# Scores of a windowed attention in eight 64x32 parts of the TensorE array, 96 keys at a time, from the third tile on

## The chip, the cores and the metric

The kernel runs on one core of one Trainium2 chip. The metric is the device time of one execution in microseconds (us). Inputs and outputs lie in the chip's memory; the host only lays the arrays out before the launch.

## What is computed

Attention over a sliding window, and a gated feed-forward layer on its output, all in float32:

```python
# q, k, v: (8 batches, 8 heads, 576 positions, 64)
scores = (q @ k.T) / sqrt(64)
mask   = (rel >= 0) & (rel < 64)            # rel = query position - key position
attn   = softmax(where(mask, scores, -1e9))
x      = (attn @ v) as 4608 tokens x 512    # the heads side by side
out    = ((sigmoid(x @ w_gate) * (x @ w_val)) @ w_out)   # 512 -> 1536 -> 512
```

A query sees itself and the 63 keys before it. So the 64 queries of one block need the keys of their own block and of the block before: 128 keys. In this 64 x 128 piece of scores only a band is kept. Its first 32 queries have nothing to keep among the last 32 keys, and its last 32 queries nothing among the first 32.

## The kernel before, in words

The 4608 tokens are cut into ten tiles: two of 384, six of 512, two of 384 (`SIZES`). A tile `t` has four pairs of heads `p` (two heads side by side on 128 partitions). One such pair in one tile is called a unit here; a unit of a 512-token tile has eight blocks of 64 queries, one of a 384-token tile six.

For each unit, `scores` multiplies each block of 64 queries with its 128 keys, for both heads: a contraction over 64 rows, 64 output rows, 128 columns. Such a product takes one quarter of the array (a 64x64 part). The four products of two neighbouring blocks and two heads lie on four different quarters and write two PSUM banks, one for each head: the row half `h` of the array always writes bank `sc[h]`. The products are float32, and the trace holds two matmul records, each with a weight load of its own, for each of them. A unit of 512 tokens thus has 32 records ahead of anything else, one of 384 tokens 24.

After the scores, VectorE reads each 128 x 128 piece from PSUM, adds a mask, scales it and takes the row minimum in one instruction (line 275, 128 columns always). ScalarE takes the exponential (line 290). Rows are divided by their sums, TensorE transposes the result (lines 382 and 395), and `outputs` multiplies it with v (line 425).

Around this runs the feed-forward layer. The first two tiles take the plain way (lines 457 and 498). The other eight go two at a time through a scheme with seven products in place of eight (`PRODUCTS`, line 659), with three instructions per product that multiply high and low parts of the operands. The weights are made in the first third of the run, written to the chip's memory and read back for each pair of tiles.

The order of TensorE's instructions is written out by hand: `put(time, order, function, ...)` fills a list of events that is sorted by time, and `pe(...)` keeps TensorE's instructions in program order. The other engines' order is planned by a list scheduler that runs a model of the timeline; `tc.issue_after` adds single constraints.

The attention of the first two tiles is done at the start, before the feed-forward layer has anything to work on. Attention of tiles three and four is done in pairs of units between the plain feed-forward stages (`near_s`, `near_h`, `near_o`). That of the later tiles is done in twelve visits of two units between the products (`far_visits`, `stage_s`). So `scores` for `t > 1` is called for two units back to back, 16 times in all: 12 times for two units of 512 tokens (64 records) and 4 times for two units of 384 tokens (48 records).

All eight PSUM banks come from pools: six with tags `b00` to `b12`, one buffer each, and one pool with two buffers (`ps_a`), which the scores, the transposed weights and some outputs share. In a visit the first unit's scores go to banks `b11` and `b01`, the second's to the two buffers of `ps_a`; the second product after the visit needs `b11` and `b01` again.

Of the kernel before, what the change touches and what calls it, by code (L numbers as in the profile page):

```python
# [9 lines left out]
F32 = mybir.dt.float32  # L10
# [6 lines left out]
PSUM = bass.MemoryType.PSUM  # L17

P = 128
BLK = 64  # L20
SMALL, BIG = 384, 512
SIZES = [SMALL] * 2 + [BIG] * 6 + [SMALL] * 2
FIRST = [sum(SIZES[:i]) for i in range(len(SIZES))]
# [2 lines left out]
def tt(t):  # L26
    return SIZES[t]


def ut(t):  # L30
    return tt(t) // BLK


def up2(t):
    return ut(t) // 2
# [3 lines left out]
def attn_ffn(ctx: ExitStack, tc: tile.TileContext, qT, kT, vS, vB, w_gate, w_val, w_out, out, outT):  # L39
# [3 lines left out]
    nc = tc.nc  # L43
    DM = out.shape[1]
    D = BLK
    NF = w_gate.shape[0]
# [5 lines left out]
    NS = NT // 2  # L52
    J_AT = [j // 2 + (j % 2) * NK for j in range(NF)]
    SCALE = 1.0 / math.sqrt(D)
    NEG = -1e9 / SCALE
    H = DM // 2
    WB, HB, RAW, CB, GB = 9, 10, 3, 3, 4
    SLOTS = 17 * 2 * BIG
# [7 lines left out]
    sm = ctx.enter_context(tc.tile_pool(name="sm", bufs=4))  # L66
    dr = ctx.enter_context(tc.tile_pool(name="dr", bufs=1, space=bass.MemoryType.DRAM))
    ps_b = ctx.enter_context(tc.tile_pool(name="ps_b", bufs=1, space=PSUM))
    ps_a = ctx.enter_context(tc.tile_pool(name="ps_a", bufs=2, space=PSUM))


    masks = {key: const.tile([P, P], F32, name=f"m_{key[0]}{key[1]}") for key in ((0, 0), (1, 0), (0, 1))}
# [2 lines left out]
    for h in range(2):  # L75
        rows = band[h * BLK:(h + 1) * BLK]
        nc.gpsimd.affine_select(out=rows, in_=rows, pattern=[[1, P]], compare_op=ALU.is_ge,
                                fill=NEG, base=-1, channel_multiplier=-1)
        nc.gpsimd.affine_select(out=rows, in_=rows, pattern=[[-1, P]], compare_op=ALU.is_ge,
                                fill=NEG, base=BLK, channel_multiplier=1)  # L80
    for h, key in enumerate(((1, 0), (0, 1))):
        nc.vector.tensor_copy(out=masks[key], in_=band)
        rows = masks[key][h * BLK:(h + 1) * BLK]
        nc.gpsimd.affine_select(out=rows, in_=rows, pattern=[[1, P]], compare_op=ALU.is_ge,
                                fill=NEG, base=-BLK, channel_multiplier=0)
    ident = const.tile([P, P], F32, name="ident")
# [2 lines left out]
    nc.vector.memset(warm, 0.0)  # L89
    nc.scalar.activation(warm, warm, AF.Exp)  # L90

    def psum(s, i, nm):
        return ps_b.tile([P, DM], F32, name=nm, tag=f"b{s % 2}{i}")

    marks = {"pT": {}}
    chain = []
# [11 lines left out]
    def pe(ins):  # L108
        return tc.keep_in_program_order(ins)
# [101 lines left out]
    def bank(t, p, n, nm):  # L211


        i = NP * t + p
        if t < 2 and i < 2 * NP - 1 and (n[0] != "s" or i % 2):
            s, x = {"s0": (0, 0), "s1": (0, 1), "p0": (1, 0), "p1": (1, 1), "o": (1 - i % 2, 2)}[n]
            return blocks(psum(s, x, nm), t)
        return blocks(ps_a.tile([P, DM], F32, name=nm, tag="a"), t)

    def blocks(bank, t):  # L220
        return bank[:, :tt(t)].rearrange("p (u c) -> p u c", u=up2(t))

    def stage_a(t, p):
        scores(t, p)
        softmax(t, p)

    def scores(t, p):
        qt, kt = ld.pop((t, p))
        if (t, p) not in sc_of:
            sc_of[(t, p)] = [bank(t, p, f"s{h}", f"s{h}_{t}_{p}") for h in range(2)]  # L230
        if (t, p) == (0, 0):
            rest = [blocks(psum(1, h, f"sb{h}_{t}_{p}"), t) for h in range(2)]
            sc_of[(t, p)] = [[x[:, 0, :]] + [y[:, u, :] for u in range(1, up2(t))] for x, y in zip(sc_of[(t, p)], rest)]
        else:
            sc_of[(t, p)] = [[x[:, u, :] for u in range(up2(t))] for x in sc_of[(t, p)]]
        sc = sc_of[(t, p)]
        for u in range(up2(t)):
            for s in range(2):
                U = 2 * u + s
                for h in range(2):  # L240
                    half = s ^ h
                    pe(nc.tensor.matmul(sc[h][u][half * BLK:(half + 1) * BLK, :],  # L242
                                     qt[h * BLK:(h + 1) * BLK, U * BLK:(U + 1) * BLK],
                                     kt[h * BLK:(h + 1) * BLK, U * BLK:U * BLK + P], start=True, stop=True))

    def softmax(t, p):
        sc = sc_of.pop((t, p))
        for h in range(2):
            exponentials(t, p, h, sc[h])
            if t < 2:  # L250
                total(t, p, h)
            else:
                normalize(t, p, h)
        if t < 2:
            stage_n(t, p)
# [53 lines left out]
    def stage_s(units, done):  # L309
        xo = []  # L310
        for i, (t, p) in enumerate(done):
            xo.append(outputs(t, p, blocks(psum(1 - i, 0, f"ob{i}_{t}_{p}"), t)))
        for i, (t, p) in enumerate(units):
            if i == 0:
                sc_of[(t, p)] = [blocks(psum(1 - h, 1, f"s{h}_{t}_{p}"), t) for h in range(2)]
            scores(t, p)
            if i == 0:
                for (dt, dp), oo in zip(done, xo):
                    x_copy(dt, dp, oo)
        if not units:  # L320
            for (dt, dp), oo in zip(done, xo):
                x_copy(dt, dp, oo)
        for i, (t, p) in enumerate(units):
            sc = sc_of.pop((t, p))
            for h in range(2):
                mn = exponentials(t, p, h, sc[h], i > 0)
                if i:
                    mn_of[(t, p, h)] = mn
# [11 lines left out]
    def by_block(x, t):  # L340
        return x[:, :tt(t)].rearrange("p (h u c) -> p h u c", h=2, u=up2(t))
# [7 lines left out]
    def near_s(units, late):  # L349
        for i, (t, p) in enumerate(units):  # L350
            if i == 0:
                sc_of[(t, p)] = [blocks(spare_bank(late, h, f"s{h}_{t}_{p}"), t) for h in range(2)]
            scores(t, p)
        for t, p in units:
            sc = sc_of.pop((t, p))
            for h in range(2):
                mn_of[(t, p, h)] = exponentials(t, p, h, sc[h], True)
# [8 lines left out]
    def near_h(units, late):  # L366
        by_halves(units, lambda r, nm: spare_bank(late, r, nm))
# [4 lines left out]

    def by_halves(units, extra=lambda r, nm: psum(1 + r, 0, nm)):
        for i, (t, p) in enumerate(units):
            pp = [extra(r, f"pp{r}_{t}_{p}") if i else ps_a.tile([P, DM], F32, name=f"pp{r}_{t}_{p}", tag="a")
                  for r in range(2)]
            for h in range(2):
                pt = st[(t, p, h)]
                for u in range(up2(t)):
                    for r in range(2):  # L380
                        rows = slice(r * BLK, (r + 1) * BLK)
                        pe(nc.tensor.transpose(by_block(pp[r], t)[:, h, u, :], pt[rows, u, :], ident[rows, rows]))  # L382
            for r in range(2):
                pT = st[(t, p, r)].rearrange("p u c -> p (u c)")
                marks["pTv"] = nc.scalar.copy(pT, pp[r][:, :tt(t)]).ins
                st[(t, p, r)] = by_block(pT, t)
            halved.add((t, p))

    def stage_b(t, p):
        UP = up2(t)  # L390
        for h in range(2):
            pt = st[(t, p, h)]
            pp = bank(t, p, f"p{h}", f"pp{h}_{t}_{p}")
            for u in range(UP):
                pe(nc.tensor.transpose(pp[:, u, :], pt[:, u, :], ident))  # L395
            if t < 2:
                pT = mp.tile([P, SMALL], F32, name=f"pT{h}_{t}_{p}", tag="g", bufs=GB).rearrange("p (u c) -> p u c", u=UP)
            else:
                pT = pt
            cp = nc.scalar.copy(pT, pp)  # L400
            marks["pTv"] = cp.ins
            if t < 2:
                marks["pT"][NP * t + p] = cp.ins
            st[(t, p, h)] = pT
# [384 lines left out]
    for n in range(2 * NP):  # L789
        t, p = divmod(n, NP)  # L790
# [123 lines left out]
    for s in range(1, NS):  # L914
# [58 lines left out]
        if s < NS - 1:  # L973
            for n in range(NPR):
                for c in range(2):
                    x = 2 * n + c
# [87 lines left out]
```

## Time and profile before

| | |
|---|---|
| median of 3 runs | 921.94 us (921.76 to 922.63) |
| span of the profiled execution, first to last instruction | 919.5 us |
| what lies around the span, against the median | 2.4 us |
| PE (TensorE matmul) busy | 907.5 us, 99% of the span |
| VectorE (DVE) busy | 679.5 us, 74% |
| ScalarE (ACT) busy | 476.1 us, 52% |

The page gives no whole time for the profiled execution beside its span, so the span stands against the median of the three runs. A busy share of TensorE near 100% says only that its queue never ran dry; how fast its matmuls follow each other has to be read stretch by stretch. Times within a trace are in us from the first instruction.

### The profile page before, as it was taken

The numbers are of one execution on the slowest core, as the hardware profiler recorded it, in microseconds if no ns is written. First come the engines' busy times: TensorE is split into PE (matmuls) and PEld (weight loads), VectorE is DVE, ScalarE is ACT, GpSimd is POOL, SyncE is SP. The second block draws the span as 40 slices with busy tenths as digits, with TensorE's granted clock in tenths as the row PEclk, the third lists the DMA queues.
The fourth block names the chain that finished last, engine by engine and source line by source line (L and its number), as shares of the span: only waits on it lengthen the run. The fifth ranks groups of instructions, "written<-read, shape, count | busy, mean of one in ns | idle before, by whom it ended". The sixth has DMA issues, their size and how long they took to land.

```text
span 919.5 us, 18434 instructions
## 1 busy us (share of the span) xinstructions
PE 907.5 (99%) x6584; PEld 788.6 (86%) x6584; DVE 679.5 (74%) x1689; ACT 476.1 (52%) x1208; POOL 129.6 (14%) x204
## 2 busy tenths in 40 slices
PE   6999999999999999999999999999999999999998
PEld 5899999888888888888888888888888888999998
DVE  7887878578898899947666698656655986565881
ACT  7867858554466677525554355424442454222550
POOL 4200000087653402001111100001110000000000
PEclk9999999999999999999999999999999999999999
DMA  9899999679989967787676665766755558888783
GB/s 338 313 406 354 359 324 358 203 244 338 345 315 331 336 241 264 253 270 243 236 233 218 206 189 193 263 217 227 228 188 172 202 187 254 270 252 251 256 256 107
DMA packets 92107, 240.02 MB, mean 261 GB/s; under 512 B 9968, under 2 KB 20080, under 8 KB 92016
## 3 DMA queue, kind: packets, MB, share of 16 engines
q1 hardware_dynamic: 91728, 238.62, 76.1%
q8 instruction: 52, 0.85, 0.4%
q14 instruction: 39, 0.32, 0.1%
q10 hardware_dynamic: 288, 0.23, 0.1%
HBM read 186.91 MB, written 51.90 MB: 260 GB/s over the span
## 4 chain that ended last, share of the span: by engine, by line
PE 97%; ACT 2%; DMA 0%; DVE 0%; issue 0%; SPq 0%; DVEq 0%; ACTq 0%
PE pr L659 47%; PE y L659 23%; PE ph L457 11%; PE y L498 6%; PE s L242 3%; PE ob L425 2%; PE pp L382 1%; PE oo L425 1%; PE pp L395 1%; ACT p L290 1%; DMA k<-in_kT_dram 0%; ACT pT L400 0%; DVE p L275 0%; SPq L195 0%; ACT w L171 0%
## 5 line engine op out<-in xcount | busy, mean ns | idle before, releaser
L659 PE MATMUL pr<-slots,wt 128*128 128x512 f32 (+1 forms) x1728 | 373.8, 375 | 0.0
L659 PEld LDWEIGHTS pr<-slots,wt 128*128 128x128 f32 x1728 | 315.3, 188 | 49.3 <-issue 1.7
L659 PE MATMUL y<-slots,wot 128*128 128x512 f32 (+1 forms) x1008 | 215.8, 375 | 0.0
L659 PEld LDWEIGHTS y<-slots,wot 128*128 128x128 f32 x1008 | 185.5, 188 | 29.6 <-issue 0.2
L465 ACT ACTIVATE g<-c 128x512 f32<-128x512 f32 (+1 forms) x72 | 43.6, 606 | 156.8 <-DVE c L698 154.5
L737 ACT CAST slots<-h 128x512 fp32r<-128x512 f32 (+1 forms) x144 | 83.7, 595 | 71.7 <-PE y L659 41.7
L290 ACT ACTIVATE p<-p,mn 128x128 f32<-128x128 f32 x288 | 108.0, 391 | 22.9 <-DVE mn L275 22.8
L738 DVE TENSOR_TENSOR slots<-h,slots 128x512 fp32r<-128x512 f32 (+1 forms) x144 | 92.9, 666 | 19.4 <-ACT slots L737 18.9
L457 PE MATMUL ph<-slots,w 128*128 128x384 f32 x576 | 104.7, 337 | 0.0
L457 PEld LDWEIGHTS ph<-slots,w 128*128 128x128 f32 x576 | 100.1, 188 | 2.1 <-DVE w L172 0.3
L305 POOL TENSOR_TENSOR p<-p,rs 128x384 f32<-128x384 f32 (+1 forms) x47 | 43.5, 946 | 346.9 <-DVE rs L298 330.7
L659 PE MATMUL pr<-slots,ws 128*128 128x512 f32 x288 | 68.3, 391 | 0.0
L669 DVE TENSOR_TENSOR c<-pr,p 128x512 f32<-128x512 f32 (+1 forms) x48 | 31.4, 655 | 45.0 <-PE pr L659 44.9
L275 DVE CUSTOM_DVE_ANT_0 p<-s,m 128x128 f32<-128x128 f32 x284 | 62.5, 285 | 1.6 <-PE s L242 1.6
L659 PEld LDWEIGHTS pr<-slots,ws 128*128 128x128 f32 x288 | 53.8, 188 | 11.0
L470 DVE SCALAR_TENSOR_TENSOR h<-g,c 128x512 f32<-128x512 f32 (+1 forms) x72 | 48.7, 676 | 6.1 <-DVE c L698 0.5
L498 PE MATMUL y<-w,slots 128*128 128x512 f32 x216 | 52.7, 396 | 0.0
L669 DVE TENSOR_TENSOR u<-pr,p 128x512 f32<-128x512 f32 (+1 forms) x48 | 31.1, 654 | 27.6 <-PE pr L659 14.8
L649 ACT CAST slots<-xf 128x512 fp32r<-128x512 f32 (+1 forms) x48 | 27.9, 598 | 40.5 <-PE y L659 31.7
L498 PEld LDWEIGHTS y<-w,slots 128*128 128x128 f32 x216 | 39.8, 188 | 8.8 <-issue 0.7
L698 DVE TENSOR_TENSOR c<-pr,p 128x512 f32<-128x512 f32 (+1 forms) x48 | 31.2, 654 | 21.3 <-PE pr L659 21.1
L290 ACT ACTIVATION_READ_ACCUMULATOR p<-p,mn 128x1 f32 x240 | 45.1, 188 | 0.0
(93 smaller groups left out, 980.7 us busy)
## 6 DMA issues: line engine op xcount, KB each, us to landing
wt<-wd SPq DMA_DIRECT2D x144, 512.0 KB, 4.3
wot<-wod SPq DMA_DIRECT2D x84, 512.0 KB, 4.2
v<-in_vB_dram SPq DMA_DIRECT2D x24, 512.0 KB, 5.5
wd<-ws SPq DMA_DIRECT2D x48, 256.0 KB, 4.5
w32d<-w SPq DMA_DIRECT2D x36, 256.0 KB, 5.4
wd<-w SPq DMA_DIRECT2D x36, 256.0 KB, 6.1
out_dram<-yo SPq DMA_DIRECT2D x30, 256.0 KB, 5.0
k<-in_kT_dram SPq DMA_DIRECT2D x24, 288.0 KB, 6.3
```

Of the source, the lines that this page charges most:

```text
L275: nc.vector.tensor_tensor_reduce(out=pt[:, u, :], in0=sc[u], in1=masks[key], op0=ALU.add, op1=ALU.min, scale=-SCALE, scalar=3.0e38, accum_ ...
L290: exp = nc.scalar.activation(pt[:, u, :], pt[:, u, :], AF.Exp, bias=mn[:, u:u + 1], scale=-1.0, **sums)
L305: eng.tensor_mul(out=pt, in0=pt, in1=rs.unsqueeze(2).broadcast_to([P, up2(t), P]))
L457: pe(nc.tensor.matmul(ph, l, r, start=i == 0 and 0 in parts, stop=i == len(prs) - 1 and NP - 1 in parts))
L465: act = nc.scalar.activation(g, c, AF.Tanh)
L470: nc.vector.scalar_tensor_tensor(out=out, in0=g, scalar=1.0, in1=val, op0=ALU.add, op1=ALU.mult)
L498: pe(nc.tensor.matmul(yb[y], l, r, start=first and n == 0, stop=last and n == 2))
L659: pe(nc.tensor.matmul(ps, l, r, start=first and i == 0, stop=last and i == 2, skip_group_check=not check))
L669: marks["plus"] = nc.vector.tensor_add(out=o, in0=ps, in1=a).ins
L698: nc.vector.tensor_add(out=c, in0=in0, in1=in1)
L737: nc.scalar.copy(h2[:, 0, :], src)
L738: lo = nc.vector.tensor_sub(out=h2[:, 1, :], in0=src, in1=h2[:, 0, :].bitcast(F32))
```

## The change

Three things are changed.

1. `scores` for `t > 1` calls `scores_by_32`. Each block of 64 queries is cut into two halves of 32, and each half is multiplied with 96 keys only: the first half with the first 96 of the 128, the second with the last 96. Each product has 32 output rows and so takes one eighth of the array (a 64x32 part). Two blocks, two heads and two halves lie on eight different parts. The 32 x 32 corners that are not written keep what the bank held before.
2. The mask value goes from -8e9 to -1e30, so that whatever lies in a corner comes out as zero after the exponential.
3. The PSUM banks are no longer taken from pools again and again. Eight tiles are made once and looked up by name; `psum_a` takes `a0` and `a1` in turn. VectorE fills the columns from 384 on of each bank with zeros at the start (eight new instructions of 128 x 128), so that nothing undefined lies there.

```diff
+Q = 32
...
-    NEG = -1e9 / SCALE
+    NEG = -1e30
...
-    ps_a = ctx.enter_context(tc.tile_pool(name="ps_a", bufs=2, space=PSUM))
...
+    banks = {x: ps_b.tile([P, DM], F32, name=f"ps_{x}") for x in [f"b{s}{i}" for s in range(2) for i in range(3)] + ["a0", "a1"]}
+    for x in banks.values():
+        nc.vector.memset(x[:, SMALL:], 0.0)
+    turn = [-1]
+
     def psum(s, i, nm):
-        return ps_b.tile([P, DM], F32, name=nm, tag=f"b{s % 2}{i}")
+        return banks[f"b{s % 2}{i}"]
+
+    def psum_a(nm):
+        turn[0] += 1
+        return banks[f"a{turn[0] % 2}"]
...
-        return blocks(ps_a.tile([P, DM], F32, name=nm, tag="a"), t)
+        return blocks(psum_a(nm), t)
...
         sc = sc_of[(t, p)]
+        if t > 1:
+            scores_by_32(t, qt, kt, sc)
+            return
...
+    def scores_by_32(t, qt, kt, sc):
+        W = P - Q
+        for u in range(up2(t)):
+            for i in range(2):
+                for s in range(2):
+                    for h in range(2):
+                        r0, c0 = (s ^ h) * BLK + i * Q, (2 * u + s) * BLK + i * Q
+                        pe(nc.tensor.matmul(sc[h][u][r0:r0 + Q, i * Q:i * Q + W], qt[h * BLK:(h + 1) * BLK, c0:c0 + Q],
+                                            kt[h * BLK:(h + 1) * BLK, c0:c0 + W], start=True, stop=True))
...
-            pp = [extra(r, f"pp{r}_{t}_{p}") if i else ps_a.tile([P, DM], F32, name=f"pp{r}_{t}_{p}", tag="a")
+            pp = [extra(r, f"pp{r}_{t}_{p}") if i else psum_a(f"pp{r}_{t}_{p}")
```

## Rows read from the trace of the kernel before

**Rows 1.** The page: busy time by engine, and the chain by line.

```profile
span 919.5 us, 18434 instructions
PE 907.5 (99%) x6584; PEld 788.6 (86%) x6584; DVE 679.5 (74%) x1689; ACT 476.1 (52%) x1208; POOL 129.6 (14%) x204
...
PE pr L659 47%; PE y L659 23%; PE ph L457 11%; PE y L498 6%; PE s L242 3%; PE ob L425 2%; PE pp L382 1%; PE oo L425 1%; PE pp L395 1%; ACT p L290 1%; DMA k<-in_kT_dram 0%; ACT pT L400 0%; DVE p L275 0%; SPq L195 0%; ACT w L171 0%
```

**Rows 2.** The chain in order of time: start, us, what.

```profile
2.12 4.39 DMA k<-in_kT_dram
...
6.64 1.62 PE s L242 x24
...
57.18 1.91 PE s L242 x64
...
244.76 1.91 PE s L242 x64
246.67 8.43 PE pr L659 x36
...
342.75 2.02 PE ob L425 x64
344.77 1.91 PE s L242 x64
...
500.13 1.47 PE s L242 x48
...
640.66 1.55 PE ob L425 x48
...
665.65 1.47 PE s L242 x48
```

**Rows 3.** Timeline of PE in three short windows around 344.70, 344.87, 345.02 us.

```profile
344.70 0.34 PE L242 MATMUL s<-k,q 64*64 64x128 f32 x4
...
344.70 0.45 PE L242 MATMUL s<-k,q 64*64 64x128 f32 x8
...
344.70 0.56 PE L242 MATMUL s<-k,q 64*64 64x128 f32 x12
```

**Rows 4.** Groups by line and shape, PE: busy us, mean ns, idle before.

```profile
L242 PE MATMUL s<-k,q 64*64 64x128 f32 x1136 | 38.9, 283 | 4.8 <-DMA k<-in_kT_dram 4.6 <-DVE rs L298 0.3
L425 PE MATMUL ob<-p,v 128*64 128x64 f32 x704 | 23.2, 224 | 0.0
```

**Rows 5.** Waits in PE's queue, lines L242 (27.50 to 27.57) and L425 (27.77 to 27.80).

```profile
L242 PEldq EVENT_SEMAPHORE  x1: 51/51/51, 27.6 to 27.6; - x1
...
L425 PEldq EVENT_SEMAPHORE  x1: 51/51/51, 27.8 to 27.8; - x1
```

**Rows 6.** Timeline of all engines, first microseconds.

```profile
0.73 0.20 POOL L74 MEMSET m<- 128x128 f32 x1 [0.29 <-POOLq L1050]
...
0.80 0.06 DVE L89 MEMSET warm<- 128x1 f32 x1 [0.80 <-PEq L1050]
...
2.64 0.46 DVE L82 COPY m<-m 128x128 f32<-128x128 f32 x2 [1.77 <-POOL m L79]
...
3.21 0.70 PE L242 MATMUL s<-k,q 64*64 64x128 f32 x8 [3.21 <-DMA k<-in_kT_dram]
...
4.08 0.29 DVE L275 CUSTOM_DVE_ANT_0 p<-s,m 128x128 f32<-128x128 f32 x1 [0.99 <-PE s L242]
```

**Rows 7.** Busy time by engine in stretches; columns PE, PEld, DVE, ACT, POOL, clock, DMA.

```profile
244.80:269.80 25.00, 25.00 (x232) 21.00 (x236) 24.80 (x70) 16.41 (x51) 15.13 (x27) 1.00 0.90 313
269.80:294.80 25.00, 25.00 (x232) 21.03 (x236) 22.44 (x65) 15.32 (x50) 10.56 (x20) 1.00 0.92 340
...
426.40:451.00 24.60, 24.60 (x250) 20.41 (x250) 16.37 (x55) 13.45 (x45) 4.08 (x4) 1.00 0.71 240
```

**Rows 8.** Timeline of DVE around 250 us: line 470 between readings of scores.

```profile
249.03 0.28 DVE L275 CUSTOM_DVE_ANT_0 p<-s,m 128x128 f32<-128x128 f32 x1
...
249.24 0.97 DVE L470 SCALAR_TENSOR_TENSOR h<-g,c 128x512 f32<-128x512 f32 x1
250.13 0.28 DVE L275 CUSTOM_DVE_ANT_0 p<-s,m 128x128 f32<-128x128 f32 x1
250.34 0.28 DVE L275 CUSTOM_DVE_ANT_0 p<-s,m 128x128 f32<-128x128 f32 x1
```

## Prediction

> **What bounds the kernel now.** I read the page first. TensorE is busy 99% of the span of 919.5 us, and the chain that ends last runs through it almost alone; the scores (line 242) have 3% of that chain [rows 1]. So a microsecond taken from TensorE's own stream comes off the end, as long as nothing that it waits for falls behind, and the most that this change can touch is those 3%.
>
> The chain in order of time gives the stretch of each visit. Two units of 512 tokens take 1.91 us for 64 records, two of 384 tokens 1.47 us for 48 [rows 2]. Of these, 12 of the first kind (from 57.18 us) and 4 of the second (the last at 665.65 us) belong to tiles from the third on: 12 x 1.91 + 4 x 1.47 = 28.8 us. That is all there is to gain from.
>
> The timeline shows how a stretch is built. In the first window four records have started, a little later eight, then twelve, and the merged end moves by 0.11 us with each four [rows 3]. So the four 64x64 parts run at the same time, and a stretch goes in rounds of four records. The chain gives the round more exactly: 1.91 - 1.47 = 0.44 us for 16 records more, four rounds, 0.110 us each. Sixteen rounds are 1.76 us, and 0.15 us is left for the ends of the stretch.
>
> **The change part by part.**
>
> *The scores.* What a round costs with 96 columns is not in the trace, but it lies between two that are. The products with v (line 425) have 64 columns and are float32 too, in two parts: 2.02 us for 64 records and 1.55 us for 48 [rows 2], so 0.47 us for eight rounds of two, 0.059 us each. From 0.059 us at 64 columns to 0.110 us at 128 it is 0.8 ns a column, so 96 columns come to 0.084 us.
>
> If all eight parts run together, two units of 512 tokens have 128 records in 16 rounds of eight: 16 x 0.084 + 0.15 = 1.49 us, 0.42 us less. Two units of 384 tokens have 12 rounds: 1.16 us, 0.31 us less. Sum: 12 x 0.42 + 4 x 0.31 = 6.3 us. The columns fall from 128 to 96 and the number of rounds stays: that is the whole gain, a quarter of the time in rounds.
>
> No row shows eight parts at once, nor four side by side in one half of the rows, so the price has to be bounded. The good end is the 6.3 us. The bad end: only four of the eight overlap, as now. Then 32 rounds of 0.084 us make 2.84 us, 0.93 us more, and 24 rounds 2.17 us, 0.70 us more: 12 x 0.93 + 4 x 0.70 = 14.0 us slower. The change breaks even when a round of eight costs what four cost now, that is when 8 x 0.084 / 0.110, about six of the eight, are in flight. I take the good end, because four parts already overlap with nothing lost: their records take 0.110 us a round against 0.059 us for half the columns, so what is paid is columns and not the number of parts.
>
> Two things could hold eight parts back. One is the weight load, since each record has one. Line 425 loads 64 columns for each of its records and still has a round of 0.059 us [rows 2, 4]; 32 columns in a round of 0.084 us are less. The other is how fast instructions come. Eight records with eight loads in 0.084 us is one pair in 10.5 ns; now it is one in 27.5 ns. The queue's own waits tell what it can do. At 27.6 us TensorE's queue passes a wait ahead of the last unit of the second tile, and at 27.8 us it has reached the wait ahead of line 425 that follows later in program order [rows 5]. The 24 pairs of that unit lie between: about 8 ns a pair, 10.4 ns at most by the window's edge and the rounding. That is enough, though not by much, and for 24 pairs and not for 128.
>
> [...]
>
> *What reads the scores.* Line 275 reads 128 columns as before, so VectorE and ScalarE have the same work. The unwritten corners cost nothing: the instruction is the same, and the mask's value changes no duration.
>
> *Where the gain meets something else.* In the visit at 244.76 us VectorE is busy 24.80 of 25.00 us [rows 7]. It reads the first unit's scores late: the first seven of its eight readings are over at 249.3 us, then an instruction of line 470 comes between, and the eighth starts at 250.13 us and ends at 250.41 us [rows 8]. The second product after the visit needs those two banks again: of the 36 records that take 8.43 us from 246.67 us on [rows 2], 12 lie ahead of the first bank, 249.5 us, and 18 ahead of the second, 250.9 us. The first bank holds the first four readings and is long free; the second has a margin of 0.5 us, and with TensorE 0.42 us earlier it is about gone. In the next stretch VectorE has 22.44 of 25.00 us, later 16.37 of 24.60 us [rows 7]; there it follows. I take 0.2 us as lost, between nothing and half of the 0.42 us in each of the five visits up to 345 us, 1.0 us.
>
> *The zeros at the start.* Eight fills of 128 x 128. VectorE's nearest row is a copy of that size, two in 0.46 us; GpSimd's own fill takes 0.20 us [rows 6]. So 8 x 0.23 = 1.84 us at most. VectorE is free from 0.86 us and idle for 1.77 us until the mask's copies at 2.64 us, TensorE first starts at 3.21 us, when a DMA lands, and the first reading of scores at 4.08 us had waited 0.99 us for TensorE [rows 6]. So the fills hide there: nothing. If they are put behind the copies instead, they end near 4.9 us and the first scores start 1.7 us late; part of that is hidden, as the chain of the first microseconds waits until 6.51 us for k by DMA [rows 2]. The bound is 1.7 us.
>
> *Fixed banks.* The same banks are used in the same order, and a bank's new writer still waits for its last reader. Neither a gain nor a loss is seen in the rows; a wait that comes earlier in one place would be at most a few tenths of a us. The planner works with other durations and may set VectorE's and ScalarE's instructions in another order; TensorE's order is fixed.
>
> Sum: -6.3 + 0.2 = -6.1 us on a span of 919.5 us, so 913.4 us. The median of the runs lies 2.4 us above the span, and so the forecast is 915.8 us.
>
> **The rivals.**
>
> *Four of eight.* The parts of one half of the rows do not all run together: up to 14.0 us slower, 936 us. For it: no row shows more than two parts side by side on the same rows. Against it: the two that are there cost each other nothing. It ends on the slow side as soon as fewer than six of eight overlap.
>
> *Starts are the limit.* Each record costs the 27.5 ns that it costs now, whatever its columns: 128 x 27.5 ns + 0.15 us = 3.67 us, 1.76 us more, and 96 records 2.79 us, 1.32 us more; together 26 us slower, 948 us. For it: no stretch shows a shorter mean distance between records. Against it: the distance is explained by columns at 64 and at 128 alike, and fours start together. [...]
>
> *The gain is not kept.* The stretches are shorter, but TensorE then waits, for VectorE's readings between 244 and 385 us, for banks, or at the start. With 1.0 us of waits and the 1.7 us at the start it is 921.9 - 6.3 + 2.7 = 918.3 us; a stall of some 0.28 us more at each of the 16 stretches, from banks or another order of the planner, adds 4.5 us, 922.8 us. For it: the margin at 250 us. Against it: elsewhere VectorE has ample room, 16.37 of 24.60 us.
>
> **How the numbers follow.** The forecast case (all eight overlap, little lost) has 0.64: 914.3 to 917.5 us, with 915.8 us as the likeliest. The lost gain has 0.16, from 917.5 to 922.8 us, half of it still more than 0.2% faster. Four of eight has 0.12, the limit on starts 0.06, and 0.02 is left for a wait that I don't see. 0.2%, 1.8 us, is about what a measurement of this kernel can tell from no change. Faster: 0.64 + 0.08 = 0.72. Within 0.2%: 0.08 and the 0.02, 0.10. Slower: 0.12 + 0.06 = 0.18. The range takes the first two cases, 0.80: 914.3 to 922.8 us.
>
> **What the profile of the changed kernel would show.** Right: the chain has 128 records of the scores in about 1.49 us and 96 in about 1.16 us; a short window shows eight records started where four stood; and eight more follow after some 0.084 us; VectorE's fills end before 3.21 us; TensorE has no new wait at 249 to 251 us. Wrong: 128 records in 2.8 us (four of eight), in 3.7 us (starts), or in 1.5 us with idle time before line 659 behind them (the gain goes into waits).

## The result, and the profile after

The changed kernel takes 931.7 us (median of 4 runs, 931.53 to 931.79) against 922.26 us for the kernel before on the same chip (4 runs, 921.76 to 922.63): 1.0102 times the time, 95% interval 1.0088 to 1.0116. It is 9.4 us slower where 6.1 us faster was forecast. The profiled execution has a span of 929.8 us, 10.3 us more than before. In every run whose span is on record the whole time lies 1.73 to 1.91 us above it, so the profiled execution of before, with a span of 919.5 us, took about 921.3 us, nearly 1 us less than its median: that is why the spans differ by more than the medians.

The page first, as in [rows 1]: busy time by engine, the instruction queue q8, the chain by engine. Line 681 is now the product of [rows 1]'s line 659, 265 the new score product, 254 the old one of the first two tiles, 447 the outputs.

```profile
PE 909.0 (98%) x7544; PEld 787.4 (85%) x7544; DVE 681.2 (73%) x1697; ACT 477.8 (51%) x1208; POOL 129.4 (14%) x204
...
q8 instruction: 60, 0.98, 0.4%
...
PE 94%; ACT 2%; DVE 2%; DMA 1%; issue 1%; ACTq 0%; DVEq 0%
```

TensorE has 960 products and 960 loads more, and 1% of the chain is now called issue: TensorE waits there for nothing that the profile shows. The chain in order of time (start, us, what) answers to [rows 2]:

```profile
256.06 0.61 DVE u L691
...
282.16 0.61 DVE u L691
...
300.80 1.19 issue
...
322.97 0.91 PE ps_b L265 x56
323.88 0.41 PE ps_a L265 x27
324.29 3.02 issue
327.31 0.89 PE ps_a L265 x31
328.20 10.79 PE ps_b L681 x36
...
436.80 1.44 issue
...
461.14 0.91 PE ps_b L265 x55
462.05 0.75 PE ps_a L265 x52
462.80 15.19 PE ps_b L681 x66
...
510.96 0.97 issue
```

Three things are to be read here. A stretch that nothing interrupts, as the one at 461.14 us, takes 1.66 us (462.80 - 461.14; the chain counts 107 of its records, the trace holds all 128) in place of 1.91 us: the gain is 0.25 us and not 0.42 us. Four pieces of issue interrupt TensorE, three of them in the middle of the scores; behind the longest, at 324.29 us, 36 products take 10.79 us in place of 8.43 us [rows 2]. And at 256 and 282 us the chain runs through VectorE's sum u (line 691: a finished product plus p1, ScalarE's copy of an earlier one). TensorE's waits in the whole span say the same (engine, line, waited for: us in total, times, longest us):

```profile
PE ps_a L265 <- issue: 5.4, 3, 3.0
...
PE ps_b L681 <- DVE u L691: 2.5, 2, 1.4
...
PE ps_b L681 <- issue: 1.2, 1, 1.2
```

So that the eight parts can be judged by themselves, here are narrow windows of the timeline as in [rows 3], all from the start of the stretch at 461.07 us to 461.16, 461.24, 461.32 and 461.40 us:

```profile
461.07 0.31 PE L265 MATMUL ps_b<-k,q 64*32 64x96 f32 x8
...
461.07 0.40 PE L265 MATMUL ps_b<-k,q 64*32 64x96 f32 x16
461.07 0.48 PE L265 MATMUL ps_b<-k,q 64*32 64x96 f32 x24
461.07 0.56 PE L265 MATMUL ps_b<-k,q 64*32 64x96 f32 x32
```

Eight products more in each 0.08 us: all eight parts run at once, and a round takes the 0.084 us of the forecast. But that holds for four rounds. In the single records the 32nd product starts 0.32 us after the first, the 33rd at 0.354 us and the 34th at 0.384 us, and from there on they come 12 ns apart; the last 95 of the 128 start over 1.10 us. The weight loads say the same: 33 of them start within 0.275 us, the 34th 0.083 us later.

What the four gaps have in common is their place in TensorE's instruction stream. The page counts 60 packets and 0.98 MB in the queue q8; the page of the kernel before has this line:

```profile
q8 instruction: 52, 0.85, 0.4%
```

That is 16.3 KB a packet in both, for 13,470 records of loads, products and waits in TensorE's stream before and 15,338 after: 259 and 256 records a packet. With TensorE's 1868 records more the queue has eight packets more; the other queue of instructions, q14, goes from 39 to 40. The first instructions behind the gaps are numbers 6081, 6593, 8385 and 10177 in that stream: 512, 1792 and 1792 apart, all multiples of 256. So the stream is counted below in blocks of 256 records, one of which begins at number 6081, and a border is the place between two blocks. Of the longest gap the window of DMA from 325.00 to 325.10 us shows what was on its way:

```profile
q8 instruction: 1, 0.02, 54.9%
```

The transfer starts at 325.02 us, 1 us into the gap, and lasts 0.88 us; TensorE goes on at 327.31 us, 1.41 us after its end. At the other three gaps it goes on 1.27, 1.45 and 1.37 us after the end of such a transfer. In all twelve traces, behind 30 us, there are 22 gaps like these of more than 0.7 us from start to start. Each stands a multiple of 256, or one record more, away from number 6081, and each ends 1.27 to 1.54 us after the end of a transfer; at the other 634 borders, counted in order with one transfer each, TensorE comes no sooner than 1.17 us after one. Of the changed kernel's 58 borders behind 30 us, 54 have no such gap; the gaps at the other four are 1.21 to 3.26 us from start to start.

### The profile page after: what moved, and what is told of

The parts are those of the page before. It is cut to its first block, busy times and chain, and to the rows that moved or that the text cites. A ratio compares the mean times of both kernels' runs of the same rounds, so it can differ in the third digit from the quotient of the medians.

```text
span 929.8 us, 20313 instructions
## 1 busy us (share of the span) xinstructions
PE 909.0 (98%) x7544; PEld 787.4 (85%) x7544; DVE 681.2 (73%) x1697; ACT 477.8 (51%) x1208; POOL 129.4 (14%) x204
## 4 chain that ended last, share of the span: by engine, by line
PE 94%; ACT 2%; DVE 2%; DMA 1%; issue 1%; ACTq 0%; DVEq 0%
PE ps_b L681 69%; PE ps_b L479 11%; PE ps_b L520 6%; PE ps_b L447 3%; PE ps_b L265 1%; PE ps_a L265 1%; ACT p L312 1%; PE ps_a L447 1%; PE ps_a L404 1%; DMA q<-in_qT_dram 1%; PE ps_a L417 1%; PE ps_b L404 1%; DVE p L297 0%; DMA k<-in_kT_dram 0%; ACT pT L422 0%
## 5 line engine op out<-in xcount | busy, mean ns | idle before, releaser
L681 PE MATMUL ps_b<-slots,wt 128*128 128x512 f32 (+1 forms) x1728 | 376.3, 376 | 1.2 <-issue 1.2
L681 PEld LDWEIGHTS ps_b<-slots,wt 128*128 128x128 f32 x1728 | 316.9, 189 | 52.6 <-ACT p L312 1.8
L681 PE MATMUL ps_b<-slots,wot 128*128 128x512 f32 (+1 forms) x1008 | 215.8, 375 | 0.0
L681 PEld LDWEIGHTS ps_b<-slots,wot 128*128 128x128 f32 x1008 | 185.5, 188 | 29.6
L479 PE MATMUL ps_b<-slots,w 128*128 128x384 f32 x576 | 104.7, 337 | 0.0
L479 PEld LDWEIGHTS ps_b<-slots,w 128*128 128x128 f32 x576 | 100.0, 188 | 2.2 <-DVE w L181 0.4
L681 PE MATMUL ps_b<-slots,ws 128*128 128x512 f32 x288 | 68.6, 391 | 2.6 <-DVE u L691 2.5
L691 DVE TENSOR_TENSOR c<-ps_b,p 128x512 f32<-128x512 f32 (+1 forms) x48 | 31.5, 656 | 47.5 <-PE ps_b L681 47.5
L681 PEld LDWEIGHTS ps_b<-slots,ws 128*128 128x128 f32 x288 | 53.7, 188 | 14.6 <-DVE u L691 2.9
L520 PE MATMUL ps_b<-w,slots 128*128 128x512 f32 x216 | 52.8, 396 | 0.0
L720 DVE TENSOR_TENSOR c<-ps_b,p 128x512 f32<-128x512 f32 (+1 forms) x48 | 31.4, 654 | 23.5 <-PE ps_b L681 23.4
```

The costliest lines, as they stand in the source:

```text
L479: pe(nc.tensor.matmul(ph, l, r, start=i == 0 and 0 in parts, stop=i == len(prs) - 1 and NP - 1 in parts))
L520: pe(nc.tensor.matmul(yb[y], l, r, start=first and n == 0, stop=last and n == 2))
L681: pe(nc.tensor.matmul(ps, l, r, start=first and i == 0, stop=last and i == 2, skip_group_check=not check))
L691: marks["plus"] = nc.vector.tensor_add(out=o, in0=ps, in1=a).ins
```

## Experiments

Two theories stood at the start. "Supply": TensorE's instructions don't come fast enough, inside a stretch and at borders of blocks. "Order": the planner moved ScalarE's copy p1 behind all of the second unit's exponentials (before, behind one or two of its last four), and with it VectorE's sum u behind both units' normalisations, and TensorE waits for u. They exclude each other only as the whole cause. The rival to both was "Banks", waits from the fixed banks. ScalarE's timeline in the visit at 244 us shows the move, first before, then in the changed kernel (COPY is p1, ACTIVATE an exponential):

```profile
253.12 0.56 ACT L674 COPY p<-pr 128x512 f32<-128x512 f32 x1
...
254.37 0.39 ACT L290 ACTIVATE p<-p,mn 128x128 f32<-128x128 f32 x1
```

```profile
253.43 0.39 ACT L312 ACTIVATE p<-p,mn 128x128 f32<-128x128 f32 x1
...
253.81 1.04 ACT L696 COPY p<-ps_b 128x512 f32<-128x512 f32 x2
```

Line numbers differ by a few from kernel to kernel: 684 and 685 below are the changed kernel's 681 (the product), 268 its 265 (the new scores), 257 its 254 (the old ones). The first four kernels ran together, beside 13 runs of before with a median of 922.01 us.

### e1_banks: everything but the scores

```
-        if t > 1:
-            scores_by_32(t, qt, kt, sc)
-            return
```

> Everything of the change but the scores: eight fixed banks, their zeros, the mask of -1e30, and the old 64x64 products over 128 columns. "Supply" (the loss comes from feeding TensorE its instructions) and "Order" (it comes from where ScalarE's copy p1 and VectorE's sums u now stand) both expect the time of before within 0.5 us, about 922.3 us, since neither the number of TensorE's instructions nor the order on the other engines differs from before but for the eight memsets. "Banks" (the fixed banks add waits that the pool did not) expects a good part of the 9.5 us here, 925 us or more.

Measured: 921.96 us (10 runs, 921.23 to 923.52), ratio 1.0002 (0.9992 to 1.0011). The fixed banks, their zeros and the mask cost nothing that these runs can tell (0.11% at most); "Banks" is out. The loss comes with the new products and with what the planner makes of them.

### e2_order: p1 and u back in their places

```
     def far_rest(t, p, sk):
...
+                with tc.issue_after(marks["p1", "0_" + sk]) if sk and h and u > 1 else nullcontext():
+                    exponential(t, p, h, u, mn_of[(t, p, h)])
...
     def stage_n(t, p, sk=None):
+        with tc.issue_after(marks["u", "0_" + sk]) if sk else nullcontext():
+            invert(sums_of[(t, p)])
```

> The changed kernel with ScalarE's copy p1 and VectorE's sums u1 held at the places among the exponentials and normalisations that they had before. "Order" as the whole cause expects about 922 us. "Order" as a part expects the gaps on u ahead of L681 (1.71, 1.29 and 0.48 us at 255.0, 281.5 and 249.5) to go and the time to fall by 2.3 to 3.2 us, to about 929 us. "Supply" expects the gaps that the chain calls issue to stay, four of 1.2 to 3.3 us or about 7 us in all, within a few instructions of where they were. If the waits on u only take the place of another wait, 931.7 us.

Measured: 930.13 us (4 runs, 927.61 to 932.74), ratio 1.0097 (1.0080 to 1.0114). TensorE's waits from 200 to 900 us in the profiled execution, which was the one of 927.61 us:

```profile
PE ps_a L265 <- issue: 4.1, 2, 2.6
PE ps_b L684 <- issue: 1.0, 1, 1.0
```

The waits on u are gone. From the stretch at 244.7 us to that at 294.7 us TensorE loses 0.2 us against before, where the changed kernel loses 2.9 us. So "Order" is right about 2.7 us, and wrong as the whole: three gaps of issue stay, ahead of the same instructions 6081, 6593 and 8385, and the fourth is replaced by one at 101.05 us, ahead of number 2241, 256 x 15 before 6081. The median fell by 1.6 us only, and the runs spread over 5.1 us where those of before spread over 1.1.

### e3_shift144: the same work, 144 instructions further on

```
+    zero = nc.const_aps.tensor(0.0, (P, 1), F32)
+    for _ in range(36):
+        tc.keep_in_program_order(nc.tensor.matmul(banks["a1"][:1, DM - 1:], zero, zero, start=True, stop=True))
```

> The changed kernel with 36 products of one zero column ahead of the first score, in the first 3 us in which TensorE waits for its first load: the same work, but each later instruction stands 144 places further on in TensorE's stream. "Supply" says that a gap comes where a border between two blocks of 256 instructions (one instruction transfer each) falls too soon behind the border before it. It expects no gap at the four old places (300.4, 324.0, 436.6 and 510.7 us), and new ones of about 1 to 3 us at the borders that now fall into the bursts at about 272, 352 and 460 us; 930 to 935 us in all. If the gaps belong to the work (a bank, an operand, a transfer of data) they stay where they are and the time is 931.7 us within 0.4.

Measured: 931.67 us (4 runs, 931.19 to 932.27), ratio 1.0104 (1.0089 to 1.0119). The timeline of TensorE in the three places that "Supply" had named (the bracket is the idle time before and its releaser):

```profile
276.12 0.53 PE L268 MATMUL ps_a<-k,q 64*32 64x96 f32 x22 [2.56 <-issue]
...
354.35 0.57 PE L268 MATMUL ps_a<-k,q 64*32 64x96 f32 x15 [2.43 <-issue]
...
464.19 0.32 PE L268 MATMUL ps_a<-k,q 64*32 64x96 f32 x2 [2.35 <-issue]
```

None of the four old gaps is left, and three new ones stand at instructions 5569, 7361 and 9153, again whole blocks of 256 apart. The gaps move with the border between blocks and not with the work. The waits on u stay (2.4 us in all), since their cause is untouched. That the time is the same is chance: three gaps of 8.1 us from start to start stand in place of four of 7.7 us, the empty products hold up the first scores until 3.96 us (3.22 us in the changed kernel), so that the stretch at 57 us starts 1.3 us later, and a lower clock (see "The clock" below) costs less: the 318 products from 354.92 us take 73.51 us where the same products take 72.31 us in the changed kernel, 1.2 us more, against 2.4 us there.

### e4_spread: the second unit's scores one product later

```
-        for i, (t, p) in enumerate(units):
+        for i, (t, p) in enumerate(units[:1]):
...
             if i:
+                put(now + visit + 0.5, 6, stage_s2, *x)
                 put(now + visit + 2.8, 6, far_rest, *x)
```

> The changed kernel with the second unit's scores of each far visit issued one product (1.4 us) later, so that 384 instructions of outputs and scores no longer come in one burst of 3.5 us. The planner then also puts p1 and u early again. "Supply" expects the issue gaps to fall from about 7 us to 1 to 4 us (blocks that hold the outputs and the first unit's scores, 256 instructions in 2.9 us, can still come too soon), "Order" the gaps on u (2.8 us) to go: together 922 to 926 us. If TensorE's gaps have another cause, 929 us (the order alone), or more if the second unit's later scores delay its exponentials.

Measured: 928.21 us (4 runs, 927.64 to 931.17), ratio 1.0073 (1.0056 to 1.0090). Waits of TensorE from 200 to 900 us:

```profile
PE ps_b L685 <- issue: 1.3, 1, 1.3
PE ps_a L265 <- issue: 1.1, 1, 1.1
```

The gaps fell as expected, from 6.6 to 2.4 us (3.0 us with one at 101 us, outside these rows), and those on u are gone, but 922 to 926 us was missed. Part of the reason is in the timeline: between a product of line 685 and the scores the starts are 0.32 us apart on the way in and 0.17 us on the way out, where two products are 0.22 us apart; a second stretch pays that a second time, about what eight parts save in a visit. And the transposes behind it wait 0.6 us for VectorE's p, which comes later too. It shows that a thinner stream helps; it does not make the change pay.

### e5_steered and e6_missteered: where the borders fall

Both are e2_order with the old products for 11 of the 32 units of tiles 2 to 9. They differ in which 11; the pairs are visit and unit, first for e5_steered:

```
+        if t > 1 and (t, p) not in WHOLE_ROWS:
             scores_by_32(t, qt, kt, sc)
...
+    WHOLE_ROWS = {unit(2 + v // NP, 2 * (v % NP) + i) for v, i in ((1, 1), (2, 1), (4, 0), (4, 1), (5, 0), (5, 1), (6, 1), (7, 1), (8, 0), (8, 1), (9, 1))}
```

In e6_missteered the first six pairs are (0, 0), (0, 1), (2, 0), (2, 1), (3, 1) and (5, 1).

> The kernel of e2_order with 21 of the 32 units (those of the first four pairs, and 13 of the 24 after them) in eight 64x32 parts and the other 11 in the old 64x64 products, chosen so that no border between blocks of 256 TensorE instructions falls less than about 4.5 us behind the one before it. "Supply" expects no issue gap after 200 us, and the gain of the shorter stretches alone, 16 x 0.125 + 5 x 0.06 = 2.3 us (from 1.91 to 1.66 us for two 512-token units): 919.7 us, between 918.9 and 920.8. If the gaps come with the eight parts wherever they stand, in proportion to their number, some 4 to 5 us of them stay and the time is 923 to 925 us.

> The same numbers of units in eight parts and in 64x64 products as in e5_steered, so the same number of instructions and of array columns, but other units, chosen so that borders fall into the bursts. "Supply" expects gaps at instructions 5313, 6337 and 6849 of TensorE's stream (counted as the trace counts its records), at about 273, 315 and 342 us, of 2.1, 1.2 and 1.6 us or up to 0.5 more each, with a lower granted clock behind the longest at most: 924 to 928 us, 4.5 us or more above e5_steered. If only the number of parts matters, the two agree within 0.5 us.

Measured, beside 17 runs of before at 921.97 us: e5_steered 922.06 us (11 runs, 921.56 to 923.88), ratio 1.0004 (0.9995 to 1.0012); e6_missteered 931.43 us (6 runs, 928.91 to 934.46), ratio 1.0104 (1.0088 to 1.0119). The same number of products and of loads, and 9.4 us between them. The chain of e6_missteered:

```profile
272.37 2.96 issue
275.33 0.40 PE ps_a L265 x15
275.73 9.98 PE ps_b L684 x36
...
327.35 2.16 issue
...
354.07 2.90 issue
```

These are the three instructions named, 5313, 6337 and 6849; the gaps are longer than expected, by about 1 us each. A fourth, of 0.8 us at 135 us, had not been named, and behind the first the granted clock is 0.50 (278 to 280 us); so the time lies above the 924 to 928 us that were expected. The one at 327.35 us stands in old 64x64 products (line 254), so it is not the shape of the new ones that stalls. e5_steered has no gap of issue after 200 us, as expected. Its gain is missing, though. A visit with one unit of each kind takes 1.96 us, more than the 1.91 us with two old ones; at 250 us VectorE holds TensorE up (see "VectorE at 250 us" below); and behind the pair at 319.7 us, which is all in eight parts, the chain runs through VectorE up to 338.67 us, where TensorE has to wait:

```profile
336.22 1.20 DVE slots L764 x2
337.42 0.60 DVE c L724
338.02 0.61 DVE c L694
338.67 4.37 PE ps_b L684 x18
```

### e7_cols48: columns or supply

```
-        W = P - Q
+        W = 48
```

> The changed kernel with 48 columns of keys a product in place of 96: half of the scores of tile 2 on is left out. If a stretch of 32 rounds is paced by its columns (0.084 us a round of eight), two units of 512 tokens take about 0.75 to 0.9 us in place of 1.66. "Supply" says that pairs of weight load and product come at 11 to 13 ns whatever their columns: 1.45 to 1.66 us, as with 96. Only this stretch is to be read, not the time.

The kernel leaves out half of the scores; its time (932.56 us, one run) says nothing. Products, loads, clock and DMA of line 265 in three parts of one stretch (start:end, us, busy of PE and PEld with their counts), first here, then in the changed kernel:

```profile
464.54:464.74 0.20, 0.20 (x32) 0.20 (x33) 1.00 0.91 369
464.74:465.24 0.50, 0.50 (x73) 0.50 (x57) 1.00 0.97 393
465.24:465.77 0.53, 0.53 (x75) 0.53 (x64) 1.00 1.00 162
```

```profile
461.07:461.48 0.41, 0.41 (x35) 0.41 (x37) 1.00 1.01 400
461.48:461.98 0.50, 0.50 (x62) 0.50 (x50) 1.00 0.63 246
461.98:462.56 0.58, 0.58 (x71) 0.58 (x56) 1.00 0.84 226
```

The counts are of instructions that lie in the part, those that reach over an edge in both. The whole stretch goes from 1.66 us to 1.36 us. Paced by columns it would have come to 0.75 to 0.9 us, so columns are not what limits it; but it is 0.1 us below what "Supply" expected. The single records tell why: the first 32 products start within 0.20 us (0.32 us with 96 columns) and the first 33 loads within 0.165 us (0.275 us), so they go by their columns; then loads pause for 0.095 us (0.083 us), and the last 95 products start over 0.93 us, 10 ns apart (1.10 us and 12 ns with 96 columns). So the first 33 pairs go at a pace that follows their columns, and the other 95 at one that hardly does. What sets the second pace is not shown; the loads themselves do not, since 33 of them start 5 ns apart here.

### e8_calm, e9_calm_shift152, e10_calm_early: a version that keeps the gain

```
+        if t in (2, 3, 8, 9) and (t, p) not in ((8, 0), (8, 2)):
             scores_by_32(t, qt, kt, sc)
...
+    for _ in range(38):
+        tc.keep_in_program_order(nc.tensor.matmul(banks["a1"][:1, :1], zero, zero, start=True, stop=True))
```

The first edit is that of all three; the loop is that of e9, e10 has it with the bank b00 in place of a1, and e8 has none.

> Eight parts only where no outputs stand in the burst (the four pairs of tiles 2 and 3) and in the last three pairs of 384 tokens, 14 of the 32 units; the old 64x64 products in tiles 4 to 7 and in the first pair of tiles 8 and 9. "Supply" expects no issue gap after 200 us and 4 x 0.25 + 3 x 0.12 to 0.26 us less TensorE time than e1_banks; "Order" expects no new wait, since VectorE and ScalarE have before's order in all of tiles 4 to 7. Together 1.4 to 1.8 us below before, 920.2 to 920.7 us. If what TensorE saves is given back at the next wait for VectorE or ScalarE, as e5_steered gave back 0.5 us behind two of its far visits, 921.5 to 922 us.

Measured: 921.99 us against 922.10 us (15 runs), ratio 0.9995 (0.9986 to 1.0004). Of 11 runs ten lie between 920.19 and 923.16 us; one of 1981.8 us stands alone, and nothing shows why. The timeline shows what took the gain of the first four stretches, a border just ahead of the last products of one of them:

```profile
169.17 0.95 PE L265 MATMUL ps_a<-k,q 64*32 64x96 f32 x60
170.68 0.32 PE L265 MATMUL ps_a<-k,q 64*32 64x96 f32 x2 [0.56 <-issue]
```

> e8_calm with 38 products of one zero column in TensorE's idle first microseconds, so that its stream stands 152 places further on and the borders of blocks fall into the middle of the bursts of tiles 2 and 3 in place of both their ends. "Supply" expects the gap of 0.8 us at 170 us to be gone and no other in its place, so the gain of 4 x 0.25 + 3 x 0.12 to 0.26 us stays: 920.2 to 920.7 us, against 921.99 for e8_calm. If the gain is given back by waits for other engines, 921.5 to 922 us again.

Measured: 921.08 us (11 runs, 920.50 to 921.56) against 922.02 us (15 runs), ratio 0.9989 (0.9980 to 0.9998). The gap is gone and no other has come. The empty products wait until 2.1 us for the last of VectorE's fills, and the first scores start 0.8 us late; but by 57 us that is hidden: the stretch there starts 0.5 us later than in before, and so it does in e8_calm, which has no empty products.

> e9_calm_shift152 with the 38 empty products written to bank b00, the first that VectorE fills with zeros, in place of a1, the last: they start at about 1.1 us in place of 2.1 and end before the first load is in. The 0.7 us by which the first scores came late in e9 should go: 920.3 to 920.5 us, against 921.08. "Supply" expects no issue gap, as in e9. If the start is hidden behind later waits of the first 57 us, 921.0 us again.

Measured: 920.69 us (11 runs, 920.09 to 921.11) against 922.10 us (14 runs, 921.21 to 923.07), ratio 0.9985 (0.9975 to 0.9994). The timeline of its first microseconds and of the stretch that had the gap in e8_calm:

```profile
1.11 2.04 PE L97 MATMUL ps_b<-const-float32-0.0 128*1 128x1 f32 x76 [1.11 <-DVE ps_b L94]
3.28 0.70 PE L257 MATMUL ps_a<-k,q 64*64 64x128 f32 x8
...
168.82 0.96 PE L268 MATMUL ps_a<-k,q 64*32 64x96 f32 x62
```

This is faster than both kernels, by 1.4 us or 0.15% of before (0.4 us by the spans of the two profiled executions). Here 14 units are in eight parts, borders still fall into their bursts, but behind 30 us none is reached less than 2.2 us after the transfer for it has ended. The earlier start is not what sets it apart from e9_calm_shift152: at 57 us the two traces stand within 0.03 us of each other. Where the 0.4 us between them come from stays open.

### The traces side by side

The start of a stretch of scores, less its start in the profiled execution of before, in us:

| stretch | after | e1_banks | e2_order | e3_shift144 | e5_steered | e6_missteered | e8_calm | e10_calm_early |
|---|---|---|---|---|---|---|---|---|
| 57.1 | +0.1 | -0.3 | +0.4 | +1.4 | 0.0 | -0.1 | +0.5 | +0.5 |
| 168.1 | -0.6 | -0.3 | +0.8 | +0.6 | -0.3 | +0.9 | +0.3 | 0.0 |
| 244.7 | -0.8 | -0.3 | +0.7 | +0.5 | -0.6 | +0.9 | +0.9 | -0.3 |
| 269.7 | +1.0 | -0.1 | +1.2 | +2.3 | -0.1 | +1.1 | +1.2 | 0.0 |
| 294.7 | +2.1 | 0.0 | +0.9 | +4.9 | 0.0 | +5.6 | +1.2 | 0.0 |
| 319.7 | +3.2 | 0.0 | +1.8 | +4.7 | 0.0 | +5.6 | +1.2 | 0.0 |
| 344.7 | +8.9 | 0.0 | +6.0 | +5.7 | +0.3 | +8.1 | +1.2 | 0.0 |
| 426.4 | +8.7 | 0.0 | +5.8 | +9.4 | +0.4 | +11.1 | +1.2 | 0.0 |
| 475.5 | +9.9 | 0.0 | +7.1 | +11.6 | +0.5 | +11.1 | +1.2 | 0.0 |
| 665.6 | +10.5 | 0.0 | +6.5 | +11.0 | +0.5 | +11.1 | +0.9 | -0.3 |

Each jump of more than 1 us upward stands behind a gap of issue or a wait on u. Where neither is, the columns are flat, fall by 0.1 to 0.3 us a stretch, or rise by up to 0.5 us, most of all behind 244.7 us. In e10_calm_early the four stretches ahead of 244.7 us gain 0.7 us, and 0.2 us of it is gone by 269.7 us.

## Why the prediction was wrong

**What bounds the kernel** held: TensorE's own stream sets the end, and what interrupts it comes out of the end in full.

**The price of a round** held: 0.08 us for eight products of 96 columns, all eight parts at once. "Four of eight" and "Starts are the limit" are both out. The second had each record at 27.5 ns; here the first eight start within 0.05 us, and 128 within 1.49 us, 11.6 ns each.

**The step that failed** is the one on how fast instructions come: 8 ns a pair over 24 pairs, "That is enough, though not by much, and for 24 pairs and not for 128." Here the first 33 pairs went by their columns (32 products started within 0.32 us with 96 columns and within 0.20 us with 48); the 95 behind them came after a pause of 0.08 to 0.1 us and 10 to 12 ns apart, with half the columns little faster than with all. That the 24 pairs were like the first 33 is likely, but not shown. That makes a stretch 1.66 us and not 1.49 us where it goes best. Stretches without a gap took 1.66 to 1.77 us in place of 1.91 us and 1.32 to 1.40 us in place of 1.47 us, on average 0.22 and 0.12 us less, so the gain of all 16 is about 12 x 0.22 + 4 x 0.12 = 3.1 us in place of 6.3 us.

**And the same step had a second half that was never asked**: how the instructions themselves come in. The change doubles the instructions of a stretch to 256, a whole block, in 1.66 us, behind 128 of the outputs in 2.02 us. In each of the 22 gaps TensorE went on 1.27 to 1.54 us after the end of a transfer. Borders close behind each other are not enough for a gap: those at 167.08 and 168.97 us of the changed kernel have no gap; the transfer for the second had ended at 166.54 us, 2.43 us before it was reached. The four gaps, start to start, are 1.58, 3.26, 1.69 and 1.21 us; less what would have passed there anyway, 7.5 us. e3_shift144 moved them to named places, and e5_steered and e6_missteered, equal in number and kind of products, differ by 9.4 us. That the borders cause them is shown. Why a transfer starts as late as it does, 1 us into the gap at 324 us, is not. The queue of data is full there (102.1% of the 16 engines' time from 324.29 to 327.31 us), but that this is the reason is only argued.

**The clock.** The prediction does not mention it, and its sums hold for a constant one. Behind the longest gap it was not constant (us, busy of PE, PEld, DVE, ACT, POOL with counts, granted clock, DMA share, GB/s):

```profile
327.40:332.10 4.70, 4.70 (x40) 3.59 (x40) 3.52 (x22) 3.53 (x19) 0.00 (x0) 0.50 0.86 315
```

The granted clock is 0.50 for these 4.7 us, after a gap of 3.26 us from start to start; from 246 to 250 us it is 1.00. The 10.79 - 8.43 = 2.4 us behind the gap are the price of that. The length of a gap alone does not decide it: in e3_shift144 the clock stayed at 1.00 behind 2.80 us at 273 us and was 0.50 (354.40 to 356.40 us) behind 2.67 us at 352 us; in e6_missteered it was 0.50 behind 3.20 us at 272 us and stayed at 1.00 behind 3.14 us at 354 us.

**The planner's order** was named and priced at nothing: "a wait that comes earlier in one place would be at most a few tenths of a us." With VectorE's readings it cost 3.3 us in the visits at 244 and 270 us, 2.7 us of which e2_order took back; the 0.6 us left are about what these readings cost in e5_steered, below. The fourth pair of products behind a visit adds to the bank that u reads, so TensorE waits for u, and u for p1. That the planner moved them because its count of TensorE's time had changed is likely, but only argued.

**VectorE at 250 us** was right in kind, down to the bank, but too small. In the chain of e5_steered TensorE goes on at 250.28 us, right behind the eighth reading (250.01 to 250.22 us), which waits for the instruction between it and the seventh (line 495 there, 470 in [rows 8]):

```profile
249.13 0.89 DVE h L495
...
250.28 4.39 PE ps_b L684 x18
```

TensorE is 0.55 us ahead of before at 244.7 us and saves 0.25 us there, and is 0.1 us ahead at 269.7 us: 0.7 us are lost, the savings of the visits before together with this one's, of which the forecast counted this one's alone. Behind 319.7 us 0.5 us more is lost. That is 1.2 us, where the forecast had 0.2 us and 1.0 us at most.

**The zeros and the fixed banks** cost nothing, as forecast: e1_banks took 921.96 us against 922.01 us.

Together: 7.5 us of gaps, 2.4 us of clock and 3.3 us of waits in two visits, less 3.1 us gained, are 10.1 of the 10.3 us by which the spans differ. The 2.4 us that the forecast put around the span were 1.73 to 1.91 us in the runs, which changes little. Of the rivals "The gain is not kept" was nearest, in the stall at some stretches and the planner's order, but its upper bound of 4.5 us was set from nothing that the trace shows.

## What to carry to other kernels

Splitting an operation into more and smaller ones had a price in instructions here, and it was paid in bursts (256 of them in 1.66 us): count how many instructions TensorE starts in a few microseconds, and compare a check of the feed only with a burst as long as the new one, since here the first 33 loads of a burst started within 0.275 us, while the last 95 of its 128 products started over 1.10 us. If a gap is called issue, count instructions from the start of the stream: here the gaps stood multiples of 256 apart and ended 1.27 to 1.54 us after a transfer of instructions. A few empty instructions at the start test it: 36 products there moved all four gaps (e3_shift144). And where a planner orders the other engines, look after any change of TensorE's work whether the instruction that TensorE waits for next still stands where it stood.

## What the runs showed of the hardware

- Eight 64x32 parts of the array run at once: rounds of eight products of 96 columns in 0.08 us, of 48 columns in about 0.05 us (32 products within 0.20 us), for the first four rounds.
- The first 33 pairs of load and product in a stretch go at that pace; behind them pairs come 10 to 12 ns apart, whether with 48 or with 96 columns.
- One packet of the instruction queue q8 is 16.3 KB, for 256 records of TensorE's stream in the changed kernel (259 before). A gap at a border lasted from 0.8 to 3.6 us (the longest in e7_cols48), and TensorE resumed 2.2 to 3.2 us after the transfer began (325.02 to 327.31 us; 435.90 to 438.24 us), 1.27 to 1.54 us after it ended.
- Two old units in one stretch take 1.91 us, two new ones 1.66 us, one of each 1.96 us. Why a mixed pair is no faster was not tried.
- Executions of some kernels with such gaps spread more: 5.1 us in e2_order, 5.6 us in e6_missteered and 3.5 us in e4_spread, against 1.0 us in e10_calm_early and 1.9 us for before beside it. The changed kernel, with 0.3 us, and e3_shift144, with 1.1 us, over four runs each, do not; why is not known.
